# Handing the eight PSUM banks to each step as the order is made, with a matmul way back and an interleaved pooled q/k tile

## The chip, the cores and the metric

The kernel runs on one core of a Trainium2 chip. The metric is the device time of that core in microseconds. The engines are called as in the profile: PE is TensorE (matmuls), PEld its weight loads, ACT is ScalarE, DVE is VectorE, POOL is GpSimd, SP is the engine that only issues DMAs. Each run comes with a state, fast or slow; ratios use fast runs only.

## The reference, cut to what matters

Eight batches of eight heads, 576 tokens, 64 columns a head. Each head gets a local attention (a band of 7 tokens) and a pooled attention (q, k and v averaged over groups of four tokens); their sum goes through two dense products with a `h - tanh(h)` between them.

```python
q_d = q.reshape(B, H, Sd, factor, D).mean(axis=3)      # factor 4, Sd = 144; k_d, v_d alike
out_up = np.repeat(sm_attn(q_d, k_d, v_d), factor, axis=2)
mask = np.abs(pos[:, None] - pos[None, :]) < factor
...                                                     # softmax over the masked scores
x = (out_up + out_local) as (4608, 512)
h = x @ w_in                                            # w_in (512, 2048)
return (h - np.tanh(h)) @ w_out                         # w_out (2048, 512)
```

## The kernel before

The kernel records its steps as operations with an engine, a duration and keys that they read and write; a small list scheduler inside the kernel then fixes the order of every engine, and the steps are emitted in that order. The framework underneath watches which steps touch which bytes (for PSUM: which banks) and puts in the semaphore waits. Heads are handled in 32 pairs; the dense work of a block of 512 tokens is woven between the attention of later pairs.

PSUM has eight banks of 512 fp32 columns. Before the change each has a fixed home: two for scores (`ps_ts`), two for outputs (`ps_ox`), and four that first serve pairs 0 to 3 and then the dense products (`ps_hy`).

```python
ps_ts = fixed("ps_ts", [128, 2, 512], FP32, pool=psum)
ps_ox = fixed("ps_ox", [128, 2, 512], FP32, pool=psum)
...
def dense_banks():
    early.close()
    pool = ctx.enter_context(tc.tile_pool(name="psum_d", bufs=1, space=PSUM))
    ps_hy.extend(fixed("ps_hy", [128, 512], FP32, 4, pool=pool))
```

The pooled q and k are written by one addition into two halves of a tile, q first and k 144 elements later:

```python
eng.tensor_tensor(out=qkd[s][:, 0:2 * G].rearrange("p (i g) -> p g i", i=2),
                  in0=half[:, :, 0, :], in1=half[:, :, 1, :], op=ALU.add)
```

After the softmax, `ln` holds the normalised outputs, tokens on partitions. The way back transposes them, copies the pooled part out of PSUM (`od`) and adds it on DVE (the prediction calls this addition the join). The first 16 pairs take this way; the later ones are transposed by DMA:

```python
def back():
    T.transpose(px[1][:, 0:128], ln[s][:, 5, :], ident)
    T.transpose(px[1][:, 128:144], ln[s][0:16, 6, :], ident[0:16, 0:16])
    for t in range(NT):
        n = NQ[t]
        T.transpose(px[0][:, QW * t:QW * t + n], ln[s][0:n, t, :], ident[0:n, 0:n])
...
op("ACT", 190, lambda: A.copy(out=od[s], in_=px[1][:, 0:144]), ...)
op("DVE", 680, lambda: V.tensor_tensor(out=xT..., in0=px[0][:, 0:576]..., in1=od[s]..., op=ALU.add), ...)
```

The softmax here doesn't subtract the row's maximum and nothing guards it: scores larger than these inputs give would overflow.

Of the kernel before, what the change touches and what calls it, by code (L numbers as in the profile page):

```python
# [14 lines left out]

class Program:
# [4 lines left out]
    def __init__(self):  # L21
        self.ops = []
        self.alternatives = {}
        self.slack = []
        self.soon = set()
        self.ring = {}
        self.rings = {}
        self.touch = []
        self.fresh = set()
        self.last_write = {}  # L30
        self.readers = {}

    def op(self, eng, ns, fn, reads=(), writes=(), pri=0, slack=0):
        i = len(self.ops)
        deps = set()
# [18 lines left out]
    def choice(self, alternatives, reads=(), writes=(), pri=0, slack=0):  # L54

        i = self.op(None, 0, None, reads, writes, pri, slack)
        self.alternatives[i] = {a[0]: a for a in alternatives}
        return i
# [29 lines left out]
    def order(self):  # L88
        n = len(self.ops)
        users = [[] for _ in range(n)]  # L90
# [7 lines left out]
        turn = {}  # L98

# [6 lines left out]
        for step in range(n):  # L106
            best = None
            for eng, cand in ready.items():
# [3 lines left out]
                if eng == "DMA":  # L112
                    pick = min((turn.get(self.ring[i][0], -1), start[self.ring[i][1]], i)
                               for i in cand if at[i] <= now)[2]
                else:
                    pick = min((self.ops[i][4], i) for i in cand if at[i] <= now)[1]
# [12 lines left out]
            end = now + self.ops[i][1]  # L129
            free[eng] = end  # L130
# [12 lines left out]
    def idle(self, order, banks, until):  # L143





        pe = [i for i in order if self.ops[i][0] == "PE" and self.start[i] < until]
        found = []  # L150
        last = 600.0
        for i in pe:
            if self.start[i] - last > 350:
                for name, keys in banks.items():
                    prev = [e for s0, e, fresh in self.uses[name] if s0 < last]
                    after = [(s0, fresh) for s0, e, fresh in self.uses[name]
                             if s0 >= last]
                    if max(prev, default=0) <= last and (not after or after[0][1]):
                        room = min(self.start[i], after[0][0] if after else until) - last
                        found.append((i, name, room))  # L160
                        break
            last = self.start[i] + self.ops[i][1]
        return found

    def emit(self, banks=None, end=None, filler=None):
        order = self.order()
        fill = {}
        if filler:
            until = min(self.start[i] for i in range(len(self.ops)) if end in self.touch[i])
            self.uses = {name: sorted(  # L170
                (self.start[i], self.start[i] + self.ops[i][1] + 200, i in self.fresh)
                for i in range(len(self.ops)) if self.touch[i] & set(keys))
                for name, keys in banks.items()}
            for i, name, room in self.idle(order, banks, until):
                slow = 430 if self.start[i] < 6000 else 230
                fill[i] = (name, int(0.75 * room / slow))
# [8 lines left out]
def kernel(  # L185
# [18 lines left out]
    A9 = 9  # L204
# [12 lines left out]
    def fixed(name, shape, dt, n=None, pool=const):  # L217
        if n is None:
# [21 lines left out]
    qkd = fixed("qkd", [128, 344], BF16, 2)  # L240
# [5 lines left out]
    warm = lT[0].rearrange("p n c -> p (n c)")[:, 0:512]  # L246
    r = fixed("r", [128, 2, 7], FP32, 2)
    ln = fixed("ln", [128, 7, 128], BF16, 2)
    od = fixed("od", [128, G], BF16, 2)
# [4 lines left out]
    ps_ts = fixed("ps_ts", [128, 2, 512], FP32, pool=psum)  # L254
    ps_ox = fixed("ps_ox", [128, 2, 512], FP32, pool=psum)
    ps_hy = []


    early = ExitStack()
    psum_e = early.enter_context(tc.tile_pool(name="psum_e", bufs=1, space=PSUM))  # L260
    ps_ts1 = fixed("ps_ts1", [128, 2, 512], FP32, pool=psum_e)
    ps_ox1 = fixed("ps_ox1", [128, 2, 512], FP32, pool=psum_e)

    sets = [(ps_ts, [("ts", 0), ("ts", 1)]), (ps_ox, ["ox"]),
            (ps_ts1, ["ts1"]), (ps_ox1, ["ox1"])]

    def dense_banks():
        early.close()
        pool = ctx.enter_context(tc.tile_pool(name="psum_d", bufs=1, space=PSUM))
        ps_hy.extend(fixed("ps_hy", [128, 512], FP32, 4, pool=pool))  # L270
# [12 lines left out]
    def c_group():  # L283
# [5 lines left out]
                         base=3, pattern=[[4, 32]], channel_multiplier=-1)  # L289

# [120 lines left out]
    def pool_v(hb):  # L411
# [3 lines left out]
        home, keys = (ps_ox, ["ox"]) if hb > 1 else sets[3 - hb]  # L415
        pv = home[:, 0, :].rearrange("p (w c) -> p w c", w=2)

        def mm():
            for t in range(NT):
                T.matmul(pv[:, 0, :], pick[:, t, :], vw[w][:, :, t, 0:64],  # L420
                         start=(t == 0), stop=(t == NT - 1))
            T.matmul(pv[:, 1, :], pick[:, 5, :], vw[w][:, :, 4, 0:64],
                     start=True, stop=True)
        P.fresh.add(len(P.ops))
        op("PE", 750, mm, reads=[("vw", w, 0), ("vw", w, 1), "pick"],
           writes=keys, pri=pri)
        op("ACT", 490, lambda: A.copy(
            out=vd[w][:, :, :, 0:64],
            in_=pv.rearrange("p w (h d) -> p w h d", d=D)),
           reads=keys, writes=[("vd", w)], pri=pri)  # L430


    def attention(p):
        b, j, hb, s, jj = p // NP, p % NP, p // 2, p % 2, p % 2
        sn, w = p % NQKN, hb % NVW
        ps, po, ts, ox = ps_ts, ps_ox, [("ts", 0), ("ts", 1)], ["ox"]
        if p < NP:
            ps, ts = sets[p]
            po, ox = ps, ts
# [23 lines left out]
        if p >= T_DMA:  # L463
# [6 lines left out]
               reads=[("qT", s)], writes=[("qk", s)], pri=pri)  # L470
        else:
            b16 = ps.rearrange("p n c -> p (n c)").bitcast(BF16)[:, 0:2 * S]

            def tr():
                for a in range(A9):
                    T.transpose(b16[:, 128 * a:128 * a + 128], qr[s][:, a, :], ident)  # L476
            P.fresh.add(len(P.ops))
            op("PE", 520 * cold, tr, slack=late, reads=[("qr", s, 0), ("qr", s, 1), "ident"],
               writes=ts, pri=pri)
            op("ACT", 1240, lambda: A.copy(  # L480
                out=full.rearrange("p (g a) i -> p g a i", a=A9),
                in_=b16.rearrange("p (a g i) -> p g a i", a=A9, i=2)),
               reads=ts, writes=[("qk", s)], pri=pri)
# [9 lines left out]
        def add2(eng):  # L493
            with nc.allow_low_precision("pooled q and k"):
                eng.tensor_tensor(out=qkd[s][:, 0:2 * G].rearrange("p (i g) -> p g i", i=2),  # L495
# [3 lines left out]
                 reads=[("qk", s)], writes=["half"], pri=pri)  # L499
# [4 lines left out]
        sc = ps.rearrange("p n c -> p (n c)")  # L504

        def score(t, hh, c, sc=sc):
            rows = slice(64 * hh, 64 * hh + 64)
            k0, q0 = LEAD + QW * t - 4, LEAD + QW * t
            T.matmul(sc[:, c:c + NQ[t]], qk[s][rows, k0:k0 + 128, 1],  # L509
                     qk[s][rows, q0:q0 + NQ[t], 0], start=p >= NP, stop=p >= NP or t >= 3)  # L510

        def biased(lo, hi):
            for hh in range(2 if p < NP else 0):
                T.matmul(ps[:, hh, 0:hi - lo], ident, bias[:, lo:hi],
                         start=True, stop=False)

        def s1():
            biased(0, 480)
            for t in range(4):
                for hh in range(2):  # L520
                    score(t, hh, 512 * hh + QW * t)

        def s2(sc=sc, step=16):
            biased(480, 576)
            for hh in range(2):
                score(4, hh, 512 * hh, sc)
            for i in range(2):
                for hh in range(2):
                    rows = slice(64 * hh, 64 * hh + 64)
                    c = 512 * hh + 96 + G * i  # L530
                    k0 = G + step * i
                    T.matmul(sc[:, c:c + G], qkd[s][rows, k0:k0 + 128],
                             qkd[s][rows, 0:G], start=True, stop=True)

        def s12():
            s1()
            s2(po.rearrange("p n c -> p (n c)"), 72)
        qks = [("qk", s)]
        yield
        new = p >= NEW  # L540
        ps2, ts2 = (po, ox) if new else (ps, ts)
        if new:
            op("PE", 620, s12, slack=late, reads=qks + [("qkd", s)], writes=ts + ox, pri=pri)
        else:
            op("PE", 420 * cold + 600 * (p < NP), s1, slack=late,
               reads=qks + ["bias"] * (p < NP), writes=ts, pri=pri)
# [4 lines left out]
            out=e1, in_=ps[:, :, 0:480], func=AF.Exp, scale=SCALE),  # L551
           reads=ts, writes=[("E", e, 0)], pri=pri)
# [6 lines left out]
        if not new:  # L559
            op("PE", 380 * cold + 150 * (p < NP), s2, slack=late, reads=qks + [("qkd", s)], writes=ts, pri=pri)  # L560
        op("ACT", 310, lambda: A.activation(  # L561
            out=e2v, in_=ps2[:, :, 0:96], func=AF.Exp, scale=SCALE),
           reads=ts2, writes=[("E", e, 1)], pri=pri)
        op("ACT", 650, lambda: A.activation(
            out=e3, in_=ps2[:, :, 96:384], func=AF.Exp, scale=SCALE / 16.0),
           reads=ts2, writes=[("E", e, 2)], pri=pri)
# [6 lines left out]


        def outs():
            for hh in range(2):
                for t in range(NT):
                    c = 480 * hh + QW * t if t < 4 else 960 + 96 * hh
                    T.matmul(po[:, hh, 65 * t:65 * t + 65], E[e][:, c:c + 128],  # L579
                             vw[w][:, 2 * jj + hh, t, :], start=True, stop=True)  # L580
                for half in range(2):
                    c = 1152 + 288 * hh + 128 * half
                    o = 65 * (NT + half)
                    for i in range(2):
                        vv = vp[s][:, hh, i, :] if new else vd[w][:, i, 2 * jj + hh, :]
                        T.matmul(po[:, hh, o:o + 65],  # L586
                                 E[e][0:vv.shape[0], c + G * i:c + G * i + 128],
                                 vv, start=(i == 0), stop=(i == 1))
        if p < NP:
            yield  # L590
            pri += 35
        P.fresh.add(len(P.ops))
# [3 lines left out]
           writes=ox, pri=pri)  # L596
        blocks = po[:, :, 0:455].rearrange("p h (n c) -> p h n c", c=65)
        op("DVE", 200, lambda: V.reciprocal(out=r[s], in_=blocks[:, :, :, 64]),
           reads=ox, writes=[("r", s)], pri=pri)
        op("DVE", 1060, lambda: V.tensor_tensor(  # L600
            out=ln[s].rearrange("p n (h d) -> p h n d", d=D),
            in0=blocks[:, :, :, 0:64],
            in1=r[s].unsqueeze(3).to_broadcast([128, 2, 7, 64]),
            op=ALU.mult), reads=ox + [("r", s)], writes=[("ln", s)], pri=pri)


        px = [po[:, i].bitcast(BF16) for i in range(2)]
# [261 lines left out]
```

## Time and profile before

| | before |
|---|---|
| time, median of 3 runs | 347.96 us (346.37 to 349.49) |
| span of the profiled run | 345.8 us |
| PE busy | 323.4 us, 94% |
| first dense matmul | 29.98 us |
| PE idle (span less busy) | 22.4 us |

This trace has 2479 matmuls for 2520 weight loads, so 41 matmul records are missing and the idle time is overstated, at 0.216 us a dense matmul by at most 8.9 us.

The head of the page, busy time of each engine, then the busy share of 40 equal slices in tenths, and the granted TensorE clock in the same slices:

```profile
span 345.8 us, 6564 instructions
PE 323.4 (94%) x2479; PEld 164.9 (48%) x2520; DVE 218.5 (63%) x336; ACT 202.7 (59%) x334; POOL 182.9 (53%) x196
...
PE   8777999999969999899989998999999999999995
...
PEclk9998999999998999999999999999999999999999
```

PE is the engine that the kernel lives on. It has a poor start (the 7s) and a few holes later. The table by stretches of 10 us shows four of the holes (columns: stretch, length, then busy time with the number of instructions for PE, PEld, DVE, ACT, POOL, then the clock, the DMA share, GB/s):

```profile
100.00:110.00 10.00, 6.41 (x60) 4.27 (x59) 6.90 (x7) 4.81 (x9) 7.97 (x9) 0.83 0.51 150
140.00:150.00 10.00, 8.40 (x53) 3.85 (x52) 8.47 (x11) 5.53 (x10) 8.40 (x9) 1.00 1.10 211
170.00:180.00 10.00, 8.56 (x81) 4.40 (x82) 9.19 (x13) 6.34 (x10) 7.49 (x9) 1.00 1.04 252
210.00:220.00 10.00, 8.62 (x67) 4.10 (x66) 7.33 (x11) 5.36 (x9) 8.18 (x8) 1.00 1.05 213
```

The timeline (start, duration, engine and line, operation; in brackets the idle time before and what ended it) shows what fills one of them:

```profile
140.41 0.72 POOL L381 CAST vw<-vst 128x640 bf16<-128x640 f32 x1
140.47 3.58 DVE L554 TENSOR_TENSOR E<-E,mask 128x960 bf16<-128x960 bf16 x1 [0.17 <-ACT E L550]
141.09 1.49 POOL L495 TENSOR_TENSOR qkd<-half 128x288 bf16<-128x288 f32 x1
142.16 1.37 POOL L448 CAST qr<-qkn 128x1152 bf16<-128x1152 f32 x1
...
144.10 0.37 PE L579 MATMUL ps_ox<-vw,E 128*128 128x65 bf16 x5 [1.54 <-DVE E L554]
```

A mask product on DVE, which takes 0.65 us when left alone, starts at 140.47 us and ends 3.58 us later, 0.52 us after the last of three POOL instructions that follow each other without a gap (it ends at 143.53). PE waits for it. In the groups (count, then busy time and mean ns of one, then idle time before) the pooled addition and the mask product stand as:

```profile
L495 POOL TENSOR_TENSOR qkd<-half 128x288 bf16<-128x288 f32 x30 | 46.0, 1535 | 3.2 <-DVE half L490 2.3
...
L554 DVE TENSOR_TENSOR E<-E,mask 128x960 bf16<-128x960 bf16 x28 | 34.1, 1216 | 14.6 <-ACT E L550 14.4
```

And the start of the dense work, with a low clock (eight matmuls in 3.46 us; at full clock eight take 1.73):

```profile
29.98 3.46 PE L661 MATMUL ps_hy<-xT,w_in_sb 128*128 128x512 bf16 x8 [1.54 <-DVE xT L641]
```

### The profile page before, as it was taken

The page shows a single profiled execution, that of the slowest core. Times are in us where ns is not written, and L with a number is a line of the kernel's source. Part 1 is how long each engine was busy: PE and PEld are TensorE (multiplying, and loading weights), DVE is VectorE, ACT ScalarE, POOL GpSimd, SP SyncE. Part 2 cuts the span into 40 slices and gives each one's busy share as a digit, 9 for nine tenths or more (in the row PEclk, how much of TensorE's full clock was granted, in tenths as well). Part 3 has the DMA queues.
Part 4 walks back from the last instruction along what each step waited for, and adds up shares of the span by engine and source line. Part 5 has one row for each costly group of instructions (what it writes and reads, how often), then busy time and mean ns, then how long its engine had stood idle before and what let it go on. Part 6 is the DMA issues. An engine that isn't in the chain of part 4 may idle for free.

```text
span 345.8 us, 6564 instructions
## 1 busy us (share of the span) xinstructions
PE 323.4 (94%) x2479; PEld 164.9 (48%) x2520; DVE 218.5 (63%) x336; ACT 202.7 (59%) x334; POOL 182.9 (53%) x196
## 2 busy tenths in 40 slices
PE   8777999999969999899989998999999999999995
PEld 3453455555535555344444444454444444444442
DVE  4775885468876775859887987776765443344300
ACT  2864875668855866576666676677654444344411
POOL 7675748577677792859786978885600100000000
PEclk9998999999998999999999999999999999999999
DMA  7999999898537892999999999662321200110021
GB/s 238 287 262 207 240 255 242 224 303 223 155 104 198 219 240 79 233 203 243 237 247 230 237 239 228 138 139 61 81 59 48 72 32 30 51 40 32 30 83 68
DMA packets 99212, 56.51 MB, mean 163 GB/s; under 512 B 77678, under 2 KB 86382, under 8 KB 99182
## 3 DMA queue, kind: packets, MB, share of 16 engines
q1 hardware_dynamic: 94670, 51.32, 60.3%
q0 software_dynamic: 4224, 4.19, 7.4%
q10 hardware_dynamic: 288, 0.59, 0.6%
q8 instruction: 19, 0.31, 0.4%
q14 instruction: 11, 0.09, 0.1%
HBM read 42.46 MB, written 9.44 MB: 150 GB/s over the span
## 4 chain that ended last, share of the span: by engine, by line
PE 80%; DVE 7%; DMA 4%; ACT 4%; issue 2%; POOL 1%; DVEq 0%; ACTq 0%; POOLq 0%
PE ps_hy L661 34%; PE ps_hy L688 31%; DVE E L554 3%; PE ps_ox L579 3%; DMA w_out_sb<-in_moe_w_out_dram 3%; PE ps_ts L509 3%; PE ps_ts L476 2%; PE ps_ox L586 2%; PE ps_ts L837 2%; DMA out_dram<-y 2%; DVE qkd L495 1%; ACT qk L480 1%; PE ps_ox L614 1%; DVE E L568 1%; PE ps_ox L420 1%
## 5 line engine op out<-in xcount | busy, mean ns | idle before, releaser
L661 PE MATMUL ps_hy<-xT,w_in_sb 128*128 128x512 bf16 x562 | 144.5, 384 | 2.7 <-DVE xT L641 1.5
L688 PE MATMUL ps_hy<-w_out_sb,gT 128*128 128x512 bf16 x550 | 138.4, 379 | 1.9 <-DMA w_out_sb<-in_moe_w_out_dram 0.5
L672 DVE TENSOR_TENSOR gT<-ps_hy,u 128x512 bf16<-128x512 f32 x144 | 97.0, 686 | 66.5 <-ACT u L669 65.5
L669 ACT ACTIVATE u<-ps_hy 128x512 f32<-128x512 f32 x144 | 85.0, 599 | 89.8 <-PE ps_hy L661 89.5
L688 PEld LDWEIGHTS <-gT 128*128 128x128 bf16 x576 | 54.0, 98 | 62.8 <-issue 0.8
L661 PEld LDWEIGHTS <-w_in_sb 128*128 128x128 bf16 x576 | 54.1, 98 | 62.6 <-issue 3.8
L495 POOL TENSOR_TENSOR qkd<-half 128x288 bf16<-128x288 f32 x30 | 46.0, 1535 | 3.2 <-DVE half L490 2.3
L490 POOL TENSOR_TENSOR half<-qk 128x576 f32<-128x576 bf16 x29 | 34.7, 1198 | 18.9 <-ACT qk L480 13.9
L554 DVE TENSOR_TENSOR E<-E,mask 128x960 bf16<-128x960 bf16 x28 | 34.1, 1216 | 14.6 <-ACT E L550 14.4
L448 POOL CAST qr<-qkn 128x1152 bf16<-128x1152 f32 x28 | 33.7, 1204 | 14.7 <-PE ps_ts L476 9.2
L600 DVE TENSOR_TENSOR ln<-ps_ox,r 128x896 bf16<-128x896 f32 x30 | 32.6, 1088 | 0.8
L699 ACT COPY y<-ps_hy 128x512 f32<-128x512 f32 x36 | 21.1, 586 | 18.4 <-PE ps_hy L688 18.4
L550 ACT ACTIVATE E<-ps_ts 128x960 bf16<-128x960 f32 x30 | 29.1, 970 | 4.6 <-PE ps_ts L509 4.6
L381 POOL CAST vw<-vst 128x640 bf16<-128x640 f32 x32 | 26.4, 826 | 2.6 <-PE ps_ox L579 2.0
L480 ACT COPY qk<-ps_ts 128x1152 bf16<-128x1152 bf16 x14 | 15.7, 1118 | 14.6 <-PE ps_ts L476 14.6
L406 POOL TENSOR_TENSOR vp<-v 72x256 bf16<-72x256 f32 x16 | 12.4, 773 | 21.1 <-PE ps_ox L586 21.1
L579 PE MATMUL ps_ox<-vw,E 128*128 128x65 bf16 x300 | 18.9, 196 | 4.2 <-DVE E L554 4.2
L579 PEld LDWEIGHTS <-E 128*128 128x128 bf16 x320 | 16.4, 99 | 11.2 <-DVE E L554 5.7
L568 DVE TENSOR_TENSOR E<-E,mask 128x192 bf16<-128x192 bf16 x28 | 17.3, 619 | 6.0 <-ACT E L561 5.7
L402 POOL TENSOR_TENSOR v<-v 72x512 f32<-72x512 f32 x16 | 20.3, 1268 | 1.0
L467 ACT COPY qk<-qT 128x1152 bf16<-128x1152 bf16 x16 | 19.3, 1207 | 0.0
L624 POOL TENSOR_TENSOR xT<-lT 128x480 bf16<-128x480 bf16 x7 | 7.1, 1009 | 23.1 <-DMA lT<-ln 23.1
(89 smaller groups left out, 254.4 us busy)
## 6 DMA issues: line engine op xcount, KB each, us to landing
vst<-in_v_dram SPq DMA_DIRECT2D x62, 160.0 KB, 4.4
qkn<-in_q_dram SPq DMA_DIRECT2D x32, 288.0 KB, 4.7
out_dram<-y SPq DMA_DIRECT2D x36, 256.0 KB, 2.0
qkn<-in_k_dram SPq DMA_DIRECT2D x30, 288.0 KB, 4.8
v<-in_v_dram SPq DMA_DIRECT2D x16, 288.0 KB
w_in_sb<-in_moe_w_in_dram POOLq DMA_DIRECT2D x4, 512.0 KB, 10.5
w_out_sb<-in_moe_w_out_dram POOLq DMA_DIRECT2D x4, 512.0 KB, 9.6
qkn<-in_k_dram ACTq DMA_DIRECT2D x2, 288.0 KB
```

Of the source, the lines that this page charges most:

```text
L381: P.choice([(eng, ns, lambda fn=fn: fn(out=vw[w][:, 2 * jj:2 * jj + 2, :, 0:64], in_=vst[s])) for eng, ns, fn in CAST_V[p >= NEARLY]], rea ...
L448: op("POOL", 1300, lambda: GP.tensor_copy(out=qr[s].rearrange("p a (h d) -> p h a d", h=2), in_=qkn[sn].rearrange("p h (a d) -> p h a d", ...
L490: eng.tensor_tensor(out=half, in0=four[:, :, 0:2, :], in1=four[:, :, 2:4, :], op=ALU.add)
L495: eng.tensor_tensor(out=qkd[s][:, 0:2 * G].rearrange("p (i g) -> p g i", i=2), in0=half[:, :, 0, :], in1=half[:, :, 1, :], op=ALU.add)
L550: op("ACT", 960, lambda: A.activation(out=e1, in_=ps[:, :, 0:480], func=AF.Exp, scale=SCALE), reads=ts, writes=[("E", e, 0)], pri=pri)
L554: op("DVE", 950, lambda: V.tensor_tensor(out=e1, in0=e1, in1=mask[:, 0:480].unsqueeze(1).to_broadcast([128, 2, 480]), op=ALU.mult), reads= ...
L579: T.matmul(po[:, hh, 65 * t:65 * t + 65], E[e][:, c:c + 128], vw[w][:, 2 * jj + hh, t, :], start=True, stop=True)
L600: op("DVE", 1060, lambda: V.tensor_tensor(out=ln[s].rearrange("p n (h d) -> p h n d", d=D), in0=blocks[:, :, :, 0:64], in1=r[s].unsqueeze( ...
L661: T.matmul(ps_hy[slot], w_in_sb[:, dc, fc * 128:(fc + 1) * 128], xT[dc][:, kb * 512:kb * 512 + 512], start=(dc == 0), stop=(dc == N_DC - 1))
L669: op("ACT", 590, lambda: A.activation(out=u[us], in_=ps_hy[slot], func=AF.Tanh), reads=[("hy", slot)], writes=[("u", us)], pri=DPRI)
L672: op("DVE", 670, lambda: V.tensor_tensor(out=gT[g][:, fc, :], in0=ps_hy[slot], in1=u[us], op=ALU.subtract), reads=[("hy", slot), ("u", us) ...
L688: T.matmul(ps_hy[slot], gT[g][:, fc, ts * 128:ts * 128 + 128], w_out_sb[:, fc, :], start=(fc == 0), stop=(fc == N_FF - 1))
```

## The change

The intent has three parts.

1. No bank has a home. All eight are one tile, and a step that fills PSUM asks for one or two banks ("Banks") when the scheduler places it; it gets those that have been free longest. After the first four pairs, attention and dense work may hold at most four each. With it the order changes: operations are ranked by their distance to the first dense block, and scores of a later pair may run before the outputs of an earlier one. Two smaller edits go with it: in the first 16 pairs the transposes of q and k and the copies of them out of PSUM are split in two, and all of the second dense product of the first block is recorded before the first product of the next (`M2_FIRST` 12 to 16).
2. The way back is done by matmuls that accumulate: the pooled part is spread over its four tokens by a matmul with a 0/1 matrix (`up`), the local part is added on top with the identity, and a plain copy takes the sum out.
3. The pooled q and k are written interleaved, as pairs.

```diff
-    ps_ts = fixed("ps_ts", [128, 2, 512], FP32, pool=psum)
-    ps_ox = fixed("ps_ox", [128, 2, 512], FP32, pool=psum)
-    ... (four more banks, handed to the dense products later)
+    bank = fixed("bank", [128, 8, 512], FP32, pool=psum)
+    def one(tok):
+        return bank[:, tok.at[0]]
+    def two(tok):
+        a, b = tok.at
+        return bank[:, a:b + 1:b - a]
...  (in the scheduler, when a step that opens a bank is placed)
+                if t.first == i:
+                    t.at = sorted(sorted((gone_at[x], x) for x in range(8)
+                                         if gone_at[x] <= now)[n][1] for n in range(t.n))
...
-            out=e1, in_=ps[:, :, 0:480], func=AF.Exp, scale=SCALE),
-           reads=ts, writes=[("E", e, 0)], pri=pri)
+            out=e1, in_=two(t1)[:, :, 0:480], func=AF.Exp, scale=SCALE),
+           drain=[t1], writes=[("E", e, 0)], pri=pri)
...
-    qkd = fixed("qkd", [128, 344], BF16, 2)
+    qkd = fixed("qkd", [128, G + 56, 2], BF16, 2)
-                eng.tensor_tensor(out=qkd[s][:, 0:2 * G].rearrange("p (i g) -> p g i", i=2),
+                eng.tensor_tensor(out=qkd[s][:, 0:G],
...
         def back():
-            T.transpose(...) x7
+            for half in range(2):
+                T.matmul(two(tb)[:, half, 0:288], ln[s][:, 5, :], up[:, 288 * half:288 * half + 288],
+                         start=True, stop=False)
+            ... (1 matmul for the last pooled tokens, 6 with the identity, all accumulating)
-        op("ACT", 190, lambda: A.copy(out=od[s], in_=px[1][:, 0:144]), ...)
-        op("DVE", 680, lambda: V.tensor_tensor(out=xT..., in0=px[0]..., in1=od[s]..., op=ALU.add), ...)
+        P.choice([("DVE", 720, lambda: V.tensor_copy(out=xs, in_=two(tb)[:, :, 0:288])),
+                  ("ACT", 680, lambda: A.copy(out=xs, in_=two(tb)[:, :, 0:288]))], drain=[tb], ...)
```

`two` is a view of two banks, a stepped view where they are not neighbours.

## The prediction

> **What bounds the kernel now.** The page has TensorE busy 94% of a 345.8 us span. The dense products are 1152 matmuls at 0.216 us (four take 0.86 us in the chain of waits), about 249 us. By the timeline:
>
> 1. Start, 0 to 29.98 us (first dense matmul). The chain of waits is vector work on the first four head pairs: three additions that write the pooled q/k tile (VectorE 1.88 and 2.18 us, GpSimd 1.50), q/k copies, join.
> 2. Dense plus attention, 29.98 to 342 us. In the table by stretches of 10 us TensorE lacks about 11 us in all; most is in four places: near 101-104 us (2.5, and the granted clock drops to 0.83), 144 (1.5), 178 and 212 us (1.4 each). Before each, a VectorE mask product of 0.24 or 0.65 us took 3.2 to 3.6 us. It has two SBUF inputs and ran beside a GpSimd sequence with the 1.5 us pooled addition. The Trainium skill, "SBUF — State Buffer", Who interferes with whom, says such a VectorE instruction contends with GpSimd reads and the loser blocks fully; the durations agree.
> 3. The last output, to 345.8 us.
>
> **Removed.** The pooled addition writes consecutive pairs instead of two far halves. From neighbours in the groups of instructions (GpSimd: 576 elements 1.2 us, 256 elements 0.77 us; VectorE: 576 elements 0.76 us) I estimate 0.8 us on GpSimd for 1.5, and 0.4 on VectorE for 2.0. The way back loses the od copy (0.28 us) and one handover; a 0.7 us copy replaces the 0.75 us join. The split q/k copy can use two engines at the start.
>
> **Added.** Way back: 9 matmuls, 1216 columns, for 7 matmuls, 720 columns. The old group took 0.62 us; I estimate +0.15 us, for the 12 pairs after the start +1.8 us. A constant on GpSimd, about 1.9 us early in the start.
>
> **Moved.** In the second half scores of pair p+1 are issued before the outputs of pair p. A late mask product then has a pair of slack, and the stalls at 144, 178 and 212 us should mostly go; outputs wait instead for banks freed by the next pair's first exponential. The start is ordered by distance to the first dense block. Loads keep their order: the fourth pair's q/k still land near 14 us.
>
> **Sum.** First dense matmul 29.98 to about 26 us: -4. Stalls after it 11 to about 7 us, and 0.7 us less at low clock: -4.7. Way back: +1.8. All lie on TensorE, the critical path. Total about -7: **341.0 us**, 8 times in 10 within **336.0 to 345.5**. Chances: faster by over 2% 0.50, within 2% 0.48, slower by over 2% 0.02.
>
> **What would show it.** Timeline: first dense matmul between 24.5 and 27.5 us. Groups: pooled addition near 0.8 us on GpSimd, under 0.6 on VectorE. Stretches: TensorE short of 10 us by over 1 us in at most two stretches after 40 us. Waits: mask product no longer the releaser of the output step.
>
> **What would make it wrong.** The weights (second quarter of w_in, later w_out) landing no earlier, so that an earlier start only turns into a wait on DMA; the pooled addition staying slow; the fixed order breaking where an engine is late, with TensorE waiting for a bank that ScalarE or VectorE has not drained; the low clock at the first dense matmuls (eight took 3.46 us) lasting longer, because fewer warm-up matmuls are issued.

## The result, and the profile after

The changed kernel took **400.93 us** (median of 3 runs, 397.23 to 403.51), against 347.96 us. A ratio here is the mean time of one kernel's fast runs over that of the other's fast runs of the same rounds, so it is not quite the ratio of the medians. This one is 1.147 (95% interval 1.130 to 1.165): slower by about 15%. The profiled run is slow (403.51 us); a second profile, fast (the run after_again below, profiled at 403.43 us), has the five PE rows of waits shown below within 0.1 us and 56.2 us in all its PE rows for 55.1, so these rows can be used.

The same head of the page:

```profile
span 401.8 us, 6709 instructions
PE 342.2 (85%) x2545; PEld 166.2 (41%) x2545; DVE 203.3 (51%) x330; ACT 206.3 (51%) x340; POOL 164.7 (41%) x199
...
PE   8779978988898858767789788897887999999995
```

PE idle time, span less busy, is 59.6 us where it was 22.4, and the holes are everywhere between 40 and 310 us: 22 of these 27 stretches of 10 us have PE busy less than 9 us. No other engine gained enough work to explain it: ACT has 206.3 us for 202.7, DVE and POOL have less. Two of the stretches (in the fast profile the clock of the first is 0.83 and not 0.67):

```profile
150.00:160.00 10.00, 7.69 (x43) 3.69 (x43) 4.80 (x7) 2.26 (x3) 5.64 (x7) 0.67 0.32 59
...
180.00:190.00 10.00, 7.17 (x74) 3.59 (x73) 4.22 (x7) 5.09 (x8) 5.62 (x7) 1.00 0.95 225
```

The view of waits (who waited for whom: us in total, times, longest) has the answer in its PE rows:

```profile
PE bank L722 <- DVE ln L660: 11.9, 10, 1.9
PE bank L722 <- ACT E L625: 5.9, 7, 1.3
PE bank L748 <- DVE ln L660: 5.7, 5, 1.9
PE bank L748 <- ACT E L610: 5.0, 6, 1.1
PE bank L748 <- ACT E L625: 4.7, 6, 1.0
```

L722 and L748 are the dense matmuls. They wait for `ln` and for the exponentials, steps of the attention, with which they share no data. All PE rows together are 55.1 us, against 15.9 us before. The other engines wait in the same odd way; here `gT`, a dense step on DVE that only reads PSUM, waits for an exponential on ACT that also only reads PSUM:

```profile
DVE gT L733 <- ACT E L625: 14.6, 8, 2.6
```

One such wait in the timeline:

```profile
182.51 0.69 DVE L733 TENSOR_TENSOR gT<-bank,u 128x512 bf16<-128x512 f32 x1 [2.61 <-ACT E L625]
...
183.39 1.09 DVE L660 TENSOR_TENSOR ln<-bank,r 128x896 bf16<-128x896 f32 x1
...
184.53 1.04 PE L748 MATMUL bank<-w_out_sb,gT 128*128 128x512 bf16 x4 [1.88 <-DVE ln L660]
```

The built program tells which banks these are. Its waits have fixed numbers, so each can be led back to the instruction that it waits for, and each instruction's banks can be read from its addresses. The matmul at 184.53 us is the 153rd of its line and writes **bank 2**; the `ln` that it waits for reads **banks 1 and 3**. Of 309 waits of PE for ACT or DVE in the changed program, 86 are of this kind: the other instruction touches two banks, the matmul's bank is neither of them and lies between them. The program before has 276 such waits for ACT or DVE, and none of this kind. 126 of the 176 two-bank instructions on ACT and DVE take banks that are not neighbours.

The pooled addition became short, as intended (1535 to 676 ns on POOL), and the mean of the mask product fell too:

```profile
L557 POOL TENSOR_TENSOR qkd<-half 128x288 bf16<-128x288 f32 x29 | 19.6, 676 | 1.9 <-DVE r L658 1.1
...
L614 DVE TENSOR_TENSOR E<-E,mask 128x960 bf16<-128x960 bf16 x28 | 26.1, 934 | 25.9 <-ACT E L610 25.9
```

The second does not follow from the first: with the same short addition the mask product has 1120 ns in x5_mixed below, and with the long one 879 ns in b3_wide.

But the dense work starts hardly earlier, at 29.39 us (30.61 in the fast profile):

```profile
29.39 1.02 PE L722 MATMUL bank<-xT,w_in_sb 128*128 128x512 bf16 x4
```

### The profile page after: what moved, and what is told of

It is laid out like the page before. It is cut to its first block, busy times and chain, and to the rows that moved or that the text cites. A ratio compares the mean times of both kernels' runs of the same rounds, so it can differ in the third digit from the quotient of the medians.

```text
span 401.8 us, 6709 instructions
## 1 busy us (share of the span) xinstructions
PE 342.2 (85%) x2545; PEld 166.2 (41%) x2545; DVE 203.3 (51%) x330; ACT 206.3 (51%) x340; POOL 164.7 (41%) x199
## 4 chain that ended last, share of the span: by engine, by line
PE 43%; DVE 9%; ACT 4%; issue 1%; ACTq 0%; DVEq 0%
PE bank L748 21%; PE bank L722 18%; DVE ln L660 3%; DVE gT L733 2%; ACT E L625 1%; PE bank L638 1%; DVE E L614 1%; PE bank L572 1%; ACT E L610 1%; PE bank L645 1%; DVE xT L691 1%; ACT u L730 1%; DVE r L658 0%; DVE xT L697 0%; ACT E L622 0%
## 5 line engine op out<-in xcount | busy, mean ns | idle before, releaser
L722 PE MATMUL bank<-xT,w_in_sb 128*128 128x512 bf16 x576 | 151.8, 384 | 21.5 <-DVE ln L660 11.9
L748 PE MATMUL bank<-w_out_sb,gT 128*128 128x512 bf16 x576 | 153.1, 385 | 19.5 <-DVE ln L660 5.7
L733 DVE TENSOR_TENSOR gT<-bank,u 128x512 bf16<-128x512 f32 x144 | 97.8, 686 | 91.4 <-ACT u L730 68.9
L730 ACT ACTIVATE u<-bank 128x512 f32<-128x512 f32 x144 | 85.6, 601 | 96.9 <-PE bank L722 87.3
L748 PEld LDWEIGHTS <-gT 128*128 128x128 bf16 x576 | 54.6, 99 | 86.8 <-issue 28.4
L722 PEld LDWEIGHTS <-w_in_sb 128*128 128x128 bf16 x576 | 53.6, 98 | 87.1 <-issue 28.3
L610 ACT ACTIVATE E<-bank 128x960 bf16<-128x960 f32 x32 | 31.3, 977 | 27.7 <-PE bank L572 8.0
L660 DVE TENSOR_TENSOR ln<-bank,r 128x896 bf16<-128x896 f32 x32 | 34.8, 1089 | 6.7 <-PE bank L748 1.4
L759 ACT COPY y<-bank 128x512 f32<-128x512 f32 x36 | 21.1, 586 | 19.8 <-PE bank L748 18.3
L625 ACT ACTIVATE E<-bank 128x576 bf16<-128x576 f32 x32 | 20.9, 652 | 10.7 <-PE bank L748 4.4
L464 POOL TENSOR_TENSOR vp<-v 72x256 bf16<-72x256 f32 x16 | 11.9, 744 | 30.3 <-PE bank L645 30.1
L638 PE MATMUL bank<-vw,E 128*128 128x65 bf16 x320 | 20.2, 197 | 4.6 <-DVE E L629 1.1
L557 POOL TENSOR_TENSOR qkd<-half 128x288 bf16<-128x288 f32 x29 | 19.6, 676 | 1.9 <-DVE r L658 1.1
## 6 DMA issues: line engine op xcount, KB each, us to landing
w_in_sb<-in_moe_w_in_dram POOLq DMA_DIRECT2D x4, 512.0 KB, 11.9
```

What stands on the lines that cost most here:

```text
L610: op("ACT", 960, lambda: A.activation(out=e1, in_=two(t1)[:, :, 0:480], func=AF.Exp, scale=SCALE), drain=[t1], writes=[("E", e, 0)], pri=pri)
L625: op("ACT", 650, lambda: A.activation(out=e3, in_=two(t2)[:, :, 96:384], func=AF.Exp, scale=SCALE / 16.0), drain=[t2], writes=[("E", e, 2) ...
L638: T.matmul(two(to)[:, hh, 65 * t:65 * t + 65], E[e][:, c:c + 128], vw[w][:, 2 * jj + hh, t, :], start=True, stop=True)
L660: op("DVE", 1060, lambda: V.tensor_tensor(out=ln[s].rearrange("p n (h d) -> p h n d", d=D), in0=blocks()[:, :, :, 0:64], in1=r[s].unsqueez ...
L722: T.matmul(one(tok), w_in_sb[:, dc, fc * 128:(fc + 1) * 128], xT[dc][:, kb * 512:kb * 512 + 512], start=(dc == 0), stop=(dc == N_DC - 1))
L730: op("ACT", 590, lambda: A.activation(out=u[us], in_=one(tok), func=AF.Tanh), drain=[tok], writes=[("u", us)], pri=DPRI)
```

## The experiments

Four theories were set against each other.

- **A.** The framework's dependence tracker takes a stepped view of banks a and b as everything from a to b. Steps then wait for readers of banks that they do not touch. The Trainium skill, "PSUM — Partial Sum Buffer", PSUM bank collisions raise a hardware error, gives a reason to be strict: two engines must not be in the same bank, on the same 32 partitions, at once, two readers included, and the compiler's scheduler puts all such pairs in order. The `gT` row above agrees with that strictness (14.6 us of a reader waiting for a reader; the built program has 25 waits of DVE for a two-bank step of ACT around DVE's bank); no run here shows the error itself.
- **B.** The new order is too tight: banks are really reused too early, and a late engine stops PE.
- **C.** The new way back and the split copies cost PE and ACT too much.
- **D.** One tile for all eight banks is itself the cause.

A fifth, that a stepped view is slower to read, is settled by the groups: `ln` takes 1089 ns on average after the change and 1088 before, the first exponential 977 and 970.

All kernels gave correct results. "PE waits" is the sum of the PE rows of the view of waits; "between" counts PE's waits for a two-bank instruction on both sides of the matmul's bank, from the built program. The profiles of after, x2_split and x6_halves are slow; the ratios are not touched by that.

| run | median us | ratio to before (95%) | PE waits us | between |
|---|---|---|---|---|
| before | 347.96 | | 15.9 | 0 |
| after | 400.93 | 1.147 (1.130 to 1.165) | 55.1 | 86 |
| after_again | 402.24 | 1.161 (1.150 to 1.172) | 56.2 | 86 |
| x1_adjacent | 342.57 | 0.990 (0.983 to 0.998) | 11.5 | 0 |
| x2_split | 339.15 | 0.978 (0.968 to 0.987) | 12.4 | 0 |
| x3_splitact | 364.89 | 1.044 (1.039 to 1.049) | 28.2 | 41 |
| x4_splitdve | 373.17 | 1.077 (1.070 to 1.085) | 34.4 | 45 |
| x5_mixed | 339.19 | 0.971 (0.967 to 0.975) | 8.7 | 0 |
| x6_halves | 347.91 | 1.003 (0.995 to 1.012) | 15.4 | 0 |
| b1_pairs | 341.29 | 0.983 (0.974 to 0.992) | 10.6 | 0 |
| b1_again | 341.53 | 0.986 (0.980 to 0.992) | 10.5 | 0 |
| b2_back | 346.55 | 1.002 (0.994 to 1.010) | 13.6 | 0 |
| b4_near | 347.64 | 0.994 (0.988 to 1.000) | 11.9 | 0 |
| b3_wide | 408.50 | 1.168 (1.160 to 1.175) | 67.9 | 66 |

### x1_adjacent: two-bank steps get neighbours

```diff
-                    t.at = sorted(sorted((gone_at[x], x) for x in range(8) if gone_at[x] <= now)[n][1] for n in range(t.n))
+            spots = sorted((max(gone_at[x:x + sizes[0]]), x) for x in range(9 - sizes[0])
+                           if all(gone_at[y] <= t and y not in taken for y in range(x, x + sizes[0])))
```

> The changed kernel, but a two-bank step gets two neighbouring banks (a, a+1). Theory A (the dependence tracker takes a strided view of banks a and b as everything from a to b, so steps wait for readers of banks that they do not touch): no such wait is left and the time is 336 to 346 us, TensorE idle under 20 us. Rival B (the order itself is too tight: real bank reuse and late engines stop TensorE): stays over 380 us. Rival C (the new way back and the split copies cost TensorE and ScalarE too much): stays over 370 us.

342.57 us, PE waits 11.5 us. As theory A has it; C falls. The rule that a step may only be placed when two neighbours are free changes the order somewhat, so against B this run alone is not clean.

### x2_split: same banks, one bank to an instruction

```diff
-            out=e1, in_=two(t1)[:, :, 0:480], func=AF.Exp, scale=SCALE),
+            lambda h: out=e1[:, h], in_=two(t1)[:, h, 0:480], ...   # for h in (0, 1)
...  (alike for the other two exponentials, the reciprocal, ln and the plain copy)
```

> The changed kernel with the same TensorE order and the same banks, but every ScalarE or VectorE instruction that reads two banks is cut into two that read one bank each. Theory A: 340 to 355 us, in spite of six more instructions a pair (about 1 us of ScalarE and VectorE a pair). Rival B (the order and the real bank reuse): as slow as the changed kernel or slower, 395 us and more, since order and banks are the same. Rival C: 400 us and more, more instructions.

339.15 us, 0.85 us below the range of theory A. PE's order and every bank number are those of the slow kernel, and ACT and DVE have more instructions (442 and 404 recorded, for 340 and 330). Only the stepped views are gone, and with them 61.8 us of the medians; B falls.

### x5_mixed: same order, neighbours where there are such

```diff
+                    near = sorted((max(gone_at[x:x + 2]), x) for x in range(7) if max(gone_at[x:x + 2]) <= now)
+                    if t.n == 2 and near:
+                        t.at = [near[0][1], near[0][1] + 1]
...
+    def each(tok, fn):                       # the few pairs left apart are read bank by bank
+        if tok.at[1] == tok.at[0] + 1:
+            fn(slice(0, 2))
+        else: ...
```

> The changed kernel with the same order on every engine; only the numbers of the banks differ: a two-bank step takes two neighbouring free banks where there are such, and the few left are read bank by bank (9 more instructions in all). Theory A: 335 to 341 us, at least as fast as x2_split, with no wait on a reader of a bank in between. Rival B (order and number of banks): as the changed kernel, 395 us and more.

339.19 us, ratio 0.971: 2.9% faster than before, and the fastest kernel against the kernel before. The order of all five engines is the same as in the slow kernel; only bank numbers differ (and 9 two-bank instructions are cut in two). Which banks a step gets, and with that whether it reads them through a stepped view, is the whole difference between 401 and 339 us. Its page and its PE waits:

```profile
PE 324.5 (96%) x2545; PEld 163.1 (48%) x2545; DVE 209.4 (62%) x332; ACT 203.4 (60%) x347; POOL 167.7 (50%) x199
```

```profile
PE bank L649 <- DVE gT L747: 1.5, 1, 1.5
PE bank L583 <- DVE ln L672: 1.4, 2, 0.8
PE bank L913 <- DVE vst L429: 1.3, 1, 1.3
```

The first dense matmul now starts at 25.57 us:

```profile
25.57 1.04 PE L736 MATMUL bank<-xT,w_in_sb 128*128 128x512 bf16 x4
```

### b4_near and b3_wide: the same fault put into the kernel before

Both are the kernel before with its eight banks as one tile and nothing else of the change. They differ in which banks the later outputs use, and which the dense products:

```diff
-    ps_ox = bank[:, 2:4]                              # b4_near
-    ps_hy = [bank[:, x] for x in (4, 5, 6, 7)]
+    ps_ox = bank[:, 2:8:5]                            # b3_wide: banks 2 and 7
+    ps_hy = [bank[:, x] for x in (3, 4, 5, 6)]
```

> Control for b3_wide: the kernel before with its eight banks as one tile, pairs of neighbours, the same order on TensorE. Theory A: as before, 345 to 350 us. Rival D (one tile for all banks is itself the cause): over 360 us.

> As b4_near and in the same order, but the pair of banks for the outputs (and, in the second half, for the pooled scores) is 2 and 7 instead of 2 and 3, with the four dense banks 3 to 6 between them. No other byte of the program's data changes. Theory A: over 370 us, dense matmuls waiting for ln and the exponentials of pairs 2 and 7. Rival B or D: as b4_near within 2 us.

347.64 us and 408.50 us. One tile is harmless (D falls), and in a kernel with the old order, the old way back and the old pooled tile the stepped view alone costs 17%. The rows of the view of waits that name `ln` as the releaser of a dense step (L652 and L679 are the dense matmuls, L660 the tanh on ACT) are, in b3_wide, with one row of an exponential below:

```profile
ACT u L660 <- DVE ln L593: 35.3, 13, 3.3
PE bank L679 <- DVE ln L593: 17.6, 14, 2.1
PE bank L652 <- DVE ln L593: 16.9, 14, 1.5
...
PE bank L652 <- ACT E L557: 8.6, 9, 1.0
```

In b4_near there is no such row; its only PE row with `ln` is the way back, which really reads it:

```profile
PE bank L603 <- DVE ln L593: 0.2, 1, 0.2
```

### x3_splitact and x4_splitdve: half the fault each

x3_splitact cuts only the exponentials on ACT bank by bank, x4_splitdve only the readers on DVE. The edits are parts of that of x2_split.

> The changed kernel with only ScalarE's exponentials cut bank by bank; VectorE still reads pairs apart. Of 86 TensorE waits on a bank in between 45 are left. Theory A: between x2_split and the changed kernel, 360 to 385 us. If the exponentials are the main cause: under 350 us; if ln is: over 390 us.

> The mirror of x3_splitact: only VectorE's readers of two banks (reciprocal, ln, the plain copy) are cut bank by bank, ScalarE's exponentials still read pairs apart. 45 TensorE waits on a bank in between are left (41 in x3_splitact, whose text gave the two numbers the wrong way round). Theory A: also between, 355 to 375 us; the two parts need not add up to the whole, since one late engine delays the other.

364.89 us with 41 waits of the kind left, and 373.17 us with 45 left. In this kernel the cost rises with the number of false waits: none 339, 41 gives 365, 45 gives 373, 86 gives 401 us. The number alone does not set it: b3_wide loses as much with 66. Neither engine's readers are the whole of it.

### b1_pairs and b1_again: only the interleaved pooled tile, in the kernel before

```diff
-    qkd = fixed("qkd", [128, 344], BF16, 2)
+    qkd = fixed("qkd", [128, G + 56, 2], BF16, 2)
-                eng.tensor_tensor(out=qkd[s][:, 0:2 * G].rearrange("p (i g) -> p g i", i=2),
+                eng.tensor_tensor(out=qkd[s][:, 0:G],
-                    T.matmul(sc[:, c:c + G], qkd[s][rows, k0:k0 + 128], qkd[s][rows, 0:G], ...)
+                    T.matmul(sc[:, c:c + G], qkd[s][rows, k0:k0 + 128, 1], qkd[s][rows, 0:G, 0], ...)
```

(To make room in SBUF `od` was laid into a tile that is idle at that time.)

> The kernel before with only the pooled q/k tile interleaved; same order of all engines. Prediction's sum: GpSimd addition 0.67 us for 1.5 (as in the changed kernel), first dense matmul 2 to 4 us earlier, the stalls behind late mask products shorter: 341 to 345 us. If the pooled addition is off the critical path: 347 to 349 us.

> b1_pairs unedited, for a tighter interval: its ratio to the kernel before was 0.983 (0.974 to 0.992), that of x5_mixed 0.971 (0.967 to 0.975). If the new banks and order of x5_mixed are worth something beyond the interleaved tile, this stays at 0.980 or above; if the tile is all of the gain, it comes to about 0.971.

341.29 and 341.53 us, ratios 0.983 and 0.986. The smallest part of the change, a few lines, gains 1.4 to 1.7% by itself. The tighter interval (0.980 to 0.992) stays above that of x5_mixed (0.967 to 0.975), so in x5_mixed the rest of the change is worth some 1.5% more. How the tile gains is only in part seen: the first dense matmul comes at 28.56 and 27.55 us for 29.98, and the 56 mask products after the start take 43.6 and 45.6 us for 51.4 (48.3 in b4_near); but one of 0.24 us still takes 3.90 us beside POOL (at 109.85 us in b1_pairs).

### b2_back: only the new way back, in the kernel before

The edit is part 2 of the change as shown above, with the fixed banks.

> The kernel before with only the new way back (9 matmuls that also add the pooled part, one copy). Prediction: TensorE +1.8 us after the start, shorter chain at the start -0.5: 348 to 350 us. Rival C (the way back costs much more): over 355 us.

346.55 us, below the expected 348 to 350; ratio 1.002 (0.994 to 1.010), no difference is shown. Rival C falls here too.

### x6_halves: x5_mixed with the pooled tile in two halves again

The edit is that of b1_pairs, backwards, in x5_mixed; PE's order and all banks stay.

> x5_mixed with the pooled q/k tile in two far halves again; the same order on TensorE, the same banks. b1_pairs gave 6 us for this part alone in the kernel before. If it adds up: 345 us. If the deeper overlap of x5_mixed already hides the slow addition, as the prediction said of the mask products: 340 to 342 us.

347.91 us, ratio 1.003: longer than both forecasts, 345 and 340 to 342 us. It more than adds up: without the interleaved tile the new banks, the new order and the new way back gain nothing, and with it they gain. In the table by stretches there are holes in x6_halves (shown first; its profile is slow) that are small or absent in x5_mixed (fast):

```profile
140.00:150.00 10.00, 6.61 (x53) 3.40 (x52) 9.89 (x8) 5.96 (x11) 8.16 (x11) 0.85 0.84 173
...
190.00:200.00 10.00, 7.55 (x63) 3.71 (x61) 8.86 (x9) 3.91 (x6) 9.05 (x11) 1.00 1.10 255
```

```profile
140.00:150.00 10.00, 10.00 (x89) 5.16 (x88) 9.13 (x11) 8.43 (x16) 9.84 (x11) 1.00 1.09 197
...
190.00:200.00 10.00, 9.10 (x68) 4.23 (x65) 9.13 (x11) 6.96 (x11) 8.10 (x8) 1.00 0.95 219
```

and the timeline of x6_halves has this in the first of them:

```profile
141.21 5.73 DVE L641 TENSOR_TENSOR E<-E,mask 128x192 bf16<-128x192 bf16 x1
...
144.58 1.54 POOL L568 TENSOR_TENSOR qkd<-half 128x288 bf16<-128x288 f32 x1
...
147.60 0.43 PE L650 MATMUL bank<-vw,E 128*128 128x65 bf16 x5 [3.39 <-DVE gT L748]
```

A mask product that alone takes 0.24 us holds DVE for 5.73 us. POOL works without a gap in that time and starts six instructions, of which the slow addition is one; a dense step behind it on DVE makes PE wait 3.39 us. That POOL is what holds it is read from such pairs of records; no run took POOL's work away. And the slow addition is not needed for such a hold: x5_mixed, with the short one, has a 0.65 us mask product that takes 3.76 us (at 158.40) beside an unbroken run of POOL:

```profile
158.40 3.76 DVE L625 TENSOR_TENSOR E<-E,mask 128x960 bf16<-128x960 bf16 x1
```

All its mask products together take 48.7 us, against 49.2 in x6_halves, so the holds alone do not account for the 8.7 us between the two kernels. In its slow profile x6_halves has 6.7 us more of PE waits, and its first dense matmul comes 2.81 us later; why the same holds cost PE more there stays open.

### after_again: the changed kernel once more

No edit.

> The changed kernel itself, unedited, on the chip of the next runs and for a profile in the fast state: 395 to 404 us, TensorE's waits again mostly for ln and the exponentials.

402.24 us, ratio 1.161; PE's waits for `ln` are 11.9 and 5.7 us as in the first profile.

One more idea, x5_mixed without the ranking by distance to the first dense block, did not build: the scheduler found no step that could be placed (presumably because every bank was held). What the ranking is worth by itself stays open.

## Why the prediction was wrong, point by point

It predicted 341.0 us within 336.0 to 345.5, and 400.93 us came. The step that failed is, in its own words, "outputs wait instead for banks freed by the next pair's first exponential", and with it the term "Stalls after it 11 to about 7 us". It took for granted that a step waits only for the banks that it uses, so its sum had no wait of a dense matmul for a reader in the attention. What the runs showed in its place: PE's waits went from 15.9 to 55.1 us, those of the dense matmuls for `ln` alone to 17.6, because 86 waits are for readers of other banks, taken as one range. With the same order and bank numbers that leave no such range the time is 339.19 us, and with the range put into the kernel before it is 408.50 us. The prediction came close to it where it named "TensorE waiting for a bank that ScalarE or VectorE has not drained", but put the risk on late engines, not on the view, and gave a slower kernel 0.02. The view `bank[:, a:b + 1:b - a]` was in the diff, and the built program's waits with their banks could have been listed before any run.

The rest, term by term:

- *"First dense matmul 29.98 to about 26 us"*: 29.39 measured. Without the false waits it is 25.57 us (x5_mixed), so the forecast of the start was right once they are gone. Without the interleaved tile it is 28.38 us (x6_halves), so most of it is the tile (one profile each, that of x6_halves slow).
- *Pooled addition "0.8 us on GpSimd for 1.5, and 0.4 on VectorE for 2.0"*: 0.68 us on POOL; on DVE three instances between 0.46 and 0.80 us, so that size was too low.
- *"Way back: +1.8"*: b2_back shows no difference, ratio 1.002, but its interval (0.994 to 1.010) is too wide to see 1.8 us, so the term is neither confirmed nor refuted.
- *"A late mask product then has a pair of slack"*: not shown to be worth much. With the slow addition and the new order (x6_halves) mask products still stop PE, by way of the dense steps queued behind them on DVE. The prediction followed one step, its inputs and its slack, and not the in-order queue behind it.
- *"TensorE short of 10 us by over 1 us in at most two stretches after 40 us"*: 22 in the changed kernel between 40 and 310 us, one in x5_mixed.
- *"the low clock at the first dense matmuls"*: the first four took 1.02 us in the first profile of the changed kernel, as in x5_mixed (1.04), and 1.79 in its second. It was no main cause.
- Not all of the loss is idle time. Between the fast profiles of x5_mixed and after_again, whose PE instructions are the same and all on record, the span grows by 63.9 us: 47.5 of PE idle time and 16.4 of more PE busy time. Part of the latter is paid at restarts: some groups of four dense matmuls that follow a wait take 1.02 to 1.04 us (as at 184.53 us above), most others 0.86. The granted clock can be another part: it is 0.83 at 150 to 160 us in after_again and 1.00 there in x5_mixed. How much each is was not separated.

## What to carry to other kernels

When buffers are handed out freely, look at how the tool that orders accesses sees the views that result: a step over two buffers that are apart can lock all that lies between. List the built program's waits, and check for each that both sides touch the same buffer. A step that needs two buffers should get neighbours; here that changed 401 to 339 us with no other edit than nine instructions cut in two. And measure the parts of a change one by one: the few lines that wrote the pooled tile in order were worth as much as the whole new bank plan, which gained nothing without them.

## What the Trainium skill lacked or had wrong

- "SBUF — State Buffer", Who interferes with whom: it says that the loser of the shared ports waits for the winner's whole instruction. The trace shows a DVE instruction that waits for a whole run of POOL instructions: a 0.65 us mask product took 3.58 us beside three of them in a row (before), one of 0.24 us took 5.73 us while six were started (x6_halves). The page has no word that a queue of POOL instructions without gaps can keep DVE out. That POOL is the cause is read from the times; no run here isolates it.
- "GPSIMD Engine Reference", 7. Performance pitfalls for Q7 kernels: it has a cost for reads with a large step, none for writes. (Other pages speak of scattered accesses in general and have figures for DVE, none for GpSimd.) The addition with the same inputs took 1.54 us when each pair of 2-byte results went to places 288 bytes apart, and 0.68 us when the pairs were written side by side (means on POOL, before and after).
- "PSUM — Partial Sum Buffer", PSUM bank collisions raise a hardware error: the rule to guard PSUM by bank is there, but not that a guard may take a stepped view of two banks as a range. It cost 17% with nothing else changed (b3_wide against b4_near, 408.50 and 347.64 us).
- "Perfetto Trace Analysis", Matmul Optimizations, advises to make use of all eight PSUM banks. The kernel before used all eight too; handing them out freely, with the new order and way back, gave nothing without the interleaved tile (x6_halves, ratio 1.003).
